# DeltaNet followed by a quick-GELU feed-forward: three feed-forward steps moved out of the second pair's hops, and dummy matmuls, conversion steps and key preparation re-dealt

## The chip, the cores and the metric

The kernel runs on one core of a Trainium2 chip. The metric is the device time of one execution in microseconds (us), as the median of several runs. A profile is one more execution with the hardware profiler on; the times inside it are counted from the start of its span.

Five engines work side by side, each through its own queue in order: TensorE (PE, matmul; its weight loads are listed apart as PEld), VectorE (DVE), ScalarE (ACT), GpSimd (POOL) and SyncE (SP, here only a queue of DMAs). They wait for each other through semaphores.

## What is computed

The reference, cut to what matters:

```python
# B, H, S, D = 4, 8, 768, 48;  d_model = H * D = 384;  d_ff = 2048
k_n = k / (norm(k, axis=-1) + 1e-6)
state = zeros((B, H, D, D))
for t in range(S):
    y[:, :, t] = q[:, :, t] @ state
    v_old = state^T k_n[:, :, t]
    state = state + beta[:, :, t] * outer(k_n[:, :, t], v[:, :, t] - v_old)
x = y.transpose(0, 2, 1, 3).reshape(B * S, H * D)       # 3072 x 384
h = x @ w_in                                            # 3072 x 2048
out = (h * sigmoid(1.702 * h)) @ w_out                  # 3072 x 384
```

So it is a recurrence over time, one per batch and head, and then a feed-forward layer on the rows that it gives. The weights w_in and w_out come in as 64-bit floats, and the kernel turns them into 32-bit floats itself.

## The kernel before

**Tiling.** Time is cut into 6 chunks of 128. A unit is a chunk and a batch: 24 units of 8 heads, numbered chunk by chunk. Inside a unit the recurrence is a triangular system, solved in 4 blocks of 32 rows. The inverses of the diagonal blocks are computed on DVE for a whole chunk (`invert`), with keys times keys (G, from PE) as input; for all chunks but the first they go out to DRAM and come back in another layout.

**Order.** All tiles that matter here are recorded through wrappers that pin an instruction to its place in the program (`pinned`, line 100), so each engine runs them in the order in which the Python code issues them. That helper has line 102, which is why the profile shows L102 nearly everywhere; groups are told apart by the tiles' names.

**Hops.** The first four units (chunk 0) are solved in two pairs (loops from lines 1021 and 1049). Each pair takes 2 x 4 hops (`hops`): in a hop one unit of the pair solves a block (psU, copied by ACT to US or U) and the other subtracts what its last solved block adds to the rows below (psR, subtracted from V by DVE). A hop needs the last hop's US and V. After a pair's hops, `put_out` computes each unit's outputs and the change of its state (psY), which ACT copies to `last` and xT and DVE adds to ST. Between a hop's instructions and those of the next hop the loops issue other work:

- `warm(n)`: n dummy matmuls of 128x256 into ps_warm, whose results nobody reads.
- `fill(n)`: n steps of the weights' conversion (`conversions`). A piece of weights takes five steps on DVE: mask the exponent into the destination (and, in the same step, a Relu on ACT that rescales it), mask the high mantissa into tmp, add the low word, join sign and exponent (this one needs the Relu), multiply. Pieces overlap by one step: the fourth step of a round begins the next piece. There are nine pieces of w_in (steps 1 to 46) and then fourteen of w_out. When a piece is done, its place may be refilled by a DMA (`fetches`).
- `ahead_of(preparing, n)`: n steps of the generator `keys`, which runs the preparation of units 4 to 8 side by side: squares on ACT (ksq), sum on DVE (ssq), a power on POOL (rn), the scaling of the keys on DVE (KN), transposes on PE (psT, copied to kT), keys times keys on PE (psG, copied to G), and the DMAs that carry G's diagonal blocks to NT (through DRAM). Here it has some 24 steps.
- `feed()`: one step of the feed-forward's first half (`hidden`): three 128x256 float matmuls (ph), which the trace shows as six; every second step also issues the gelu (gT) on ACT. The first two `hidden` take 32 feeds in all.

**Behind the hops** comes the second inverse (`inverting = invert(1)`, line 1086): 25 times a step of it and a feed, then what is left of both, then conversion steps (line 1091). Then `woven` runs over the remaining units: each call issues one step of up to three units at different stages, and spends a share of a queue of feed-forward work. The first thing in that queue is `both_written` (line 771), the second half of the feed-forward for the first two units' rows (po); it runs through w_out in sixteen parts and calls `fill` itself until the parts that it is about to need have been converted.

**PSUM.** psU, psR and psY share the four banks of ps_seq, taken in turn; psT and psG (of chunk 1) share the two of ps_big; ps_warm, ph and po the two of ps_moe.

Of the kernel before, what the change touches and what calls it, by code (L numbers as in the profile page):

```python
# [18 lines left out]
def kernel(  # L19
# [35 lines left out]
    GB = 8  # L55

    XR = DP - D
    NW, NA, NY, NU = 14, 3, 34, 11
    NQ = DFF // 4
    NPC = DFF // 8  # L60
    NS = C * C + C
# [22 lines left out]
    def load(n, pairs, dma=nc.sync.dma_start):  # L84
        c, b = units[n]
        for dst, src in pairs:
            dma(
                out=dst[n % len(dst)][:, :, 0:D],
                in_=src[b, :, c * C : (c + 1) * C, :].rearrange("h p d -> p h d"),
            )  # L90

    def load_values(n, dma=nc.sync.dma_start):
        c, b = units[n]
        V = io.tile([128, H, D], F32, tag="V", name="V", bufs=4)
        dma(
            out=V, in_=v[b, :, c * C : (c + 1) * C, :].rearrange("h p d -> p h d")
        )
        loaded[n] = V
# [33 lines left out]
    def warm(n):  # L132
        ps = ps_moe.tile([128, 256], F32, tag="moe", name="ps_warm")
        for _ in range(n):
            pe.matmul(ps, lhsT=ones[:, 0:128], rhs=ones, start=True, stop=True)
# [52 lines left out]
    def fetch_out(f):  # L188

        if f in outside:  # L190
            slot = outside[f]
            if slot not in slots:
                slots[slot] = wk.tile([128, 2 * DM], I32, tag=slot[:2].strip("2"), name="raw", bufs=3)
            words = slots[slot]
        else:
            words = raws[:, inside[f] * DM : (inside[f] + 2) * DM]
        places[f] = as_raw(words, (1, DM))
        first = order.index(f) < FC // 2
        (other_queue if first else sync)(
            out=as_rows(places[f])[:, 0], in_=moe_w_out[f * 128 : (f + 1) * 128, :]  # L200
        )
# [90 lines left out]
    def fill(n):  # L292
        for _ in range(n):
            next(converting, None)
# [459 lines left out]
    def written(c, b0, gT):  # L754

        for i in range(HB):
            b = b0 + i
            po = ps_moe.tile([128, DM], F32, tag="moe", name="po")
            for f in range(FC):
                pe.matmul(  # L760
                    po, lhsT=gT[f // FQ][:, f % FQ, i * C : (i + 1) * C], rhs=w_out[:, f, :],
                    start=(f == 0), stop=(f == FC - 1),
                )
                if f % 2 == 1 and f < FC - 1:
                    yield 1.3
            o = wk.tile([128, DM], F32, tag="o", name="o")
            act.copy(o, po)
            nc.sync.dma_start(out=out[b * S + c * C : b * S + (c + 1) * C, :], in_=o)
            yield 1.3

    def both_written(c, gT):

        po = [ps_moe.tile([128, DM], F32, tag="moe", name="po") for _ in range(HB)]
        for n, f in enumerate(order):
            ahead = order[min(n + 3, FC - 1)]
            while ("out", ahead - ahead % 2 if 4 <= ahead < 8 else ahead) not in done:
                fill(1)
            for i in range(HB):
                pe.matmul(
                    po[i], lhsT=gT[f // FQ][:, f % FQ, i * C : (i + 1) * C], rhs=w_out[:, f, :],  # L780
                    start=(n == 0), stop=(n == FC - 1),
                )
            if n < FC - 1:
                yield 1.3
        for i in range(HB):
            o = wk.tile([128, DM], F32, tag="o", name="o")
            act.copy(o, po[i])
            sync(out=out[i * S + c * C : i * S + (c + 1) * C, :], in_=o)
        yield 1.3
# [11 lines left out]
    def run(work):  # L801
        for _ in work:
            pass

    def ahead_of(work, n):
        for _ in range(n):
            next(work, None)
# [18 lines left out]
    def together(solves, belows):  # L826

        solves = [(X, blk) for X, blk in solves if X]
        belows = [(X, blk) for X, blk in belows if X]
        psU = bank("psU") if solves else None  # L830
        psR = bank("psR") if belows else None
        for h in range(H):
            for X, blk in solves:
                X.solve(blk, h, psU)
            for X, blk in belows:
                X.below(blk, h, psR)
        for X, blk in solves:
            X.solved(blk, psU)
        for X, blk in belows:
            X.rest(blk, psR)  # L840
# [157 lines left out]
    def keys():  # L998

        def unit(n):  # L1000
            yield from normalize_mixed(n)
            yield from prepare(n)

        begun[2 * B] = prepare(2 * B)

        def first(n):
            yield from normalize_mixed(n)
            next(begun[n])

        work = [unit(n) for n in range(B, 2 * B)] + [first(2 * B)]  # L1010
        for t in range(24):
            for u, begin in reversed(list(enumerate((0, 3, 6, 10, 13)))):
                s = t - begin
                if s >= 0 and s % 2 == 0:
                    next(work[u], None)
            yield
        for w in work:
            run(w)

    preparing = keys()  # L1020
    path = hops(*pair[:2])
    for i in range(2 * NB):
        together(*next(path))
        fill(2)
        if i in (3, 5):
            pair[HB + (i - 3) // 2].select()
        if i > 0:
            ahead_of(preparing, 1)
        warm(NU if i < 6 else NA)
    for n, s in enumerate(pair[:2]):  # L1030
        put_out(s, 2 - n)
        load(len(KN) + n, ((KN, k),), other_queue)
# [4 lines left out]
    def feed(n=1):  # L1037
        for _ in range(n):
            while ffn and next(ffn[0], None) is None:
                ffn.pop(0)  # L1040
# [9 lines left out]
    for i in range(2 * NB):  # L1050
        together(*next(path))
        fill(2 if i < 5 else 3)
        if i > 2:
            feed()
        else:
            warm(NU)
        ahead_of(preparing, 2)
        if 3 <= i < 6:
            fetch_out(i - 3)
        if i == 5:  # L1060
            load(B, ((QP, q),), sync)
            load_values(B, sync)
# [25 lines left out]
        ahead_of(inverting, 1)  # L1088
        feed()
    run(inverting)  # L1090
    fill(5)
    while ffn:
        feed()
    queue = [both_written(0, gTs[0]), written(*units[HB], gTs[1])]
    for n in range(B - 1, len(units) + 1):
        woven(n, 20.8 if n > 6 else 10.4)
# [32 lines left out]
```

## Time and profile before

| | us |
|---|---|
| median of 8 runs | 775.46 (773.9 to 776.14) |
| profiled execution | 775.92 |
| its span | 774.2 |
| PE busy | 750.4 (97%) |
| DVE busy | 440.5 (57%) |
| ACT busy | 240.9 (31%) |
| POOL busy | 128.5 (17%) |

Stages of the profiled execution, by the timeline of PE:

| stage | from, us | to, us |
|---|---|---|
| dummies ahead of the first hop (34) | 37.9 | 43.6 |
| first pair's hops | 43.6 | 62.9 |
| first pair's put-outs | 65.2 | 69.9 |
| second pair's hops | 69.8 | 93.9 |
| second pair's put-outs, first scores of unit 4 | 93.9 | 104.1 |
| 25 feeds (150 ph) beside the second inverse | 104.1 | 136.8 |
| second half of the feed-forward and further units | 136.6 | 774.2 |

How to read the profile: "busy" is the time in which an engine executes; matmuls are pipelined and their ends are modelled. In the row of digits the span is cut into 40 slices. In a timeline a row gives the start, the duration, the engine, the operation, what it writes and reads and how many instructions were merged; the bracket is how long the engine had been idle before and which engine's instruction ended that. PEclk is the clock granted to TensorE, 1.00 being full speed.

### The profile page before, as it was taken

Reading aid. Unit: us, or ns where it says so; the run is one execution under the profiler, and the core shown is the slowest. Engines: PE = TensorE matmul, PEld = TensorE weight load, DVE = VectorE, ACT = ScalarE, POOL = GpSimd, SP = SyncE. Lnnn points to the kernel's source line nnn. Section 1 sums busy time; section 2 is a strip of 40 time slices with the busy share of each in tenths; the row PEclk is TensorE's granted clock in tenths of the full one; section 3 lists DMA queues with packets and bytes.
Section 4 is the critical chain, followed back from the end, with each engine's and each line's share of the span. In section 5 each row is a group of like instructions: output and inputs, shape, how many; then the busy total and the mean of one; then the engine's idle time right before and its main releaser. Section 6 shows DMA issues by size and latency. Waiting matters only on the chain.

```text
span 774.2 us, 19538 instructions
## 1 busy us (share of the span) xinstructions
PE 750.4 (97%) x8537; PEld 563.6 (73%) x8537; DVE 440.5 (57%) x896; ACT 240.9 (31%) x535; POOL 128.5 (17%) x134
## 2 busy tenths in 40 slices
PE   7898999789999999999999999999999999999998
PEld 6677788456688678678678678678678677687684
DVE  6979788896965565665665665666665621000000
ACT  4564632343333223223233233223123123121110
POOL 6124210110220320220221221231210000000000
PEclk7598999999999999999999999999999999999999
DMA  9956551454342142042042042042030020000000
GB/s 158 176 73 187 120 100 33 120 131 97 76 109 56 25 105 56 22 108 57 22 99 65 22 99 65 22 99 66 22 77 12 22 44 1 17 12 1 26 1 20
DMA packets 130661, 50.78 MB, mean 66 GB/s; under 512 B 105408, under 2 KB 126016, under 8 KB 130576
## 3 DMA queue, kind: packets, MB, share of 16 engines
q1 hardware_dynamic: 128112, 41.08, 24.7%
q0 software_dynamic: 2464, 8.46, 4.5%
q8 instruction: 67, 1.10, 0.6%
q14 instruction: 18, 0.15, 0.1%
HBM read 32.08 MB, written 16.25 MB: 62 GB/s over the span
## 4 chain that ended last, share of the span: by engine, by line
PE 87%; DVE 7%; ACT 3%; DMA 2%; issue 1%; SPq 0%; DVEq 0%; ACTq 0%
PE ph L102 31%; PE po L102 30%; PE psY L102 6%; PE psU L102 5%; PE psQ L102 4%; PE psG L102 4%; PE psT L102 3%; PE psR L102 3%; DVE w_out L102 2%; DVE tmp L102 2%; ACT V L102 1%; PE ps_warm L102 1%; DVE P L102 1%; DVE V L102 1%; DMA KN<-in_k_dram 1%
## 5 line engine op out<-in xcount | busy, mean ns | idle before, releaser
L102 PE MATMUL po<-w_out,gT 128*128 128x384 f32 x768 | 267.5, 496 | 5.5 <-DVE w_out L102 5.5
L102 PE MATMUL ph<-xT,w_in 128*128 128x256 f32 x1152 | 261.1, 383 | 0.3
L102 PEld LDWEIGHTS ph<-xT,w_in 128*128 128x128 f32 x1152 | 214.9, 190 | 32.7 <-issue 1.7
L102 PEld LDWEIGHTS po<-w_out,gT 128*128 128x128 f32 x768 | 142.0, 192 | 97.2 <-DVE w_out L102 8.2
L102 DVE TENSOR_TENSOR V<-V,psR 128x384 f32<-128x384 f32 (+2 forms) x72 | 40.1, 557 | 195.7 <-PE psR L102 191.2
L102 ACT ACTIVATE gT<-ph 128x512 f32<-128x512 f32 x96 | 56.5, 596 | 144.8 <-PE ph L102 144.7
L102 DVE TENSOR_TENSOR P<-NT,YB 64x8 f32<-64x8 f32 (+26 forms) x178 | 86.4, 486 | 4.9
L102 PEld LDWEIGHTS psU<-V,XB 32*32 32x32 f32 x1536 | 59.0, 105 | 35.3 <-issue 27.6
L102 ACT COPY US<-psU 32x384 f32<-32x384 f32 x92 | 43.1, 469 | 133.0 <-PE psR L102 80.1
L102 DVE TENSOR_REDUCE YB<-P 64x4 f32<-64x8 f32 (+27 forms) x178 | 77.2, 434 | 6.1
L102 PE MATMUL psU<-V,XB 32*32 32x48 f32 x1536 | 70.4, 204 | 2.3 <-DVE V L102 2.1
L624 POOL TENSOR_SCALAR_AFFINE_SELECT M<-M 128x1024 f32<-128x1024 f32 x20 | 25.5, 1276 | 231.3 <-DVE M L102 169.3
L102 PE MATMUL psR<-US,G 32*32 32x48 f32 x2576 | 62.7, 204 | 0.9 <-ACT US L102 0.9
L102 PEld LDWEIGHTS psR<-US,G 32*32 32x32 f32 x2576 | 53.3, 104 | 2.4 <-ACT US L102 1.3
L102 PE MATMUL psQ<-QS,kT 48*128 48x176 f32 (+1 forms) x384 | 37.6, 341 | 3.7 <-ACT QS L102 3.7
L102 DVE TENSOR_TENSOR P<-NT 64x256 f32<-64x256 f32 (+7 forms) x44 | 36.3, 826 | 0.5
L102 DVE TENSOR_REDUCE NT<-P 64x64 f32<-64x1024 f32 (+7 forms) x44 | 35.3, 803 | 1.5
L102 PEld LDWEIGHTS psQ<-QS,kT 48*128 48x128 f32 x384 | 31.1, 209 | 6.8 <-ACT QS L102 5.5
L102 PE MATMUL psG<-kT 48*128 48x128 f32 x384 | 33.0, 311 | 2.7 <-ACT kT L102 1.4
L102 PEld LDWEIGHTS psG<-kT 48*128 48x128 f32 x384 | 28.0, 210 | 6.2 <-ACT G L102 2.1
L102 ACT COPY o<-po 128x384 f32<-128x384 f32 x24 | 11.5, 477 | 62.0 <-issue 39.2
L102 ACT COPY M<-psQ 128x256 f32<-128x256 f32 x68 | 22.8, 377 | 22.9 <-DVE V L102 16.8
(100 smaller groups left out, 602.7 us busy)
## 6 DMA issues: line engine op xcount, KB each, us to landing
Nd<-G SPq DMA_DIRECT2D x16, 512.0 KB, 3.5
QP<-in_q_dram SPq DMA_DIRECT2D x24, 192.0 KB, 3.8
V<-in_v_dram SPq DMA_DIRECT2D x24, 192.0 KB, 3.2
out_dram<-o SPq DMA_DIRECT2D x24, 192.0 KB, 2.4
KN<-in_k_dram POOLq DMA_DIRECT2D x15, 192.0 KB, 3.6
NT<-Nd SPq DMA_DIRECT2D x20, 128.0 KB, 2.7
Yd<-YS SPq DMA_DIRECT2D x20, 128.0 KB, 2.4
XB<-Yd SPq DMA_DIRECT2D x20, 128.0 KB, 3.4
```

What stands on the lines that cost most here:

```text
L102: return lambda *a, **kw: tc.keep_in_program_order(op(*a, **kw))
L624: (pool if self.n < B else nc.gpsimd).affine_select(out=self.M, in_=self.M, compare_op=ALU.is_gt, fill=0.0, base=0, pattern=[[0, H], [1, 1 ...
```

## The change

It does five things. Of the dummies, 26 instead of 34 go ahead of the first hop, the last two hops of the first pair get eleven each instead of three, and in the second pair hops 0 to 5 get seven each, where hops 0 to 2 had eleven. The first hop gets five conversion steps instead of two. The feeds of hops 3, 4 and 5 of the second pair are left out; they are issued after the second inverse. Hops 2 to 5 of the second pair take three steps of the keys' preparation instead of two. And the five conversion steps after the second inverse are replaced by three behind each of the feeds that are left there; with the closing turn, which finds no feed, these are twelve.

```diff
-    NW, NA, NY, NU = 14, 3, 34, 11
+    NW, NY, NU = 14, 26, 11
...
     path = hops(*pair[:2])
     for i in range(2 * NB):
         together(*next(path))
-        fill(2)
+        fill(2 if i else 5)
         if i in (3, 5):
             pair[HB + (i - 3) // 2].select()
         if i > 0:
             ahead_of(preparing, 1)
-        warm(NU if i < 6 else NA)
+        warm(NU)
...
     for i in range(2 * NB):
         together(*next(path))
         fill(2 if i < 5 else 3)
-        if i > 2:
+        if i > 5:
             feed()
         else:
-            warm(NU)
-        ahead_of(preparing, 2)
+            warm(NU * 2 // 3)
+        ahead_of(preparing, 3 if 2 <= i < 6 else 2)
...
     run(inverting)
-    fill(5)
     while ffn:
         feed()
+        fill(3)
```

## The prediction

> **What bounds the kernel now.** I read the busy slices of the page first, then the chain of waits, then clock windows, then the timelines of single engines between 42 and 176 us. Each slice below is 19.4 us, each digit a tenth.
>
> ```profile
> PE   7898999789999999999999999999999999999998
> DVE  6979788896965565665665665666665621000000
> PEclk7598999999999999999999999999999999999999
> PE 87%; DVE 7%; ACT 3%; DMA 2%; issue 1%; SPq 0%; DVEq 0%; ACTq 0%
> ```
>
> From about 176 us on TensorE (PE) sets the time without a gap, and the change touches nothing there: whatever is won or lost before 176 us arrives at the end one for one. So the question is how early the last w_out pieces are converted. The chain before that is mixed: VectorE (DVE) sets it in the first pair's hops (49 to 62 us), PE in the put-outs and the second pair's hops (62 to 104 us), PE's 25 feed-forward steps during the second inverse (104.1 to 136.8 us), then DVE converting w_out until 172 us.
>
> The granted clock (columns: PE, PEld, DVE, ACT, POOL busy; PEclk; DMA):
>
> ```profile
> 58.70:62.10 3.40, 1.44 (x35) 0.95 (x34) 3.27 (x7) 0.72 (x2) 0.18 (x1) 1.00 0.87 223
> 147.40:150.80 3.40, 1.75 (x7) 0.83 (x8) 3.26 (x7) 1.17 (x2) 0.00 (x0) 1.00 0.44 120
> 62.10:65.50 3.40, 3.39 (x27) 2.74 (x29) 3.37 (x5) 1.77 (x3) 1.31 (x1) 0.51 0.88 196
> 65.50:68.90 3.40, 3.40 (x43) 3.40 (x43) 2.71 (x5) 1.57 (x5) 1.54 (x2) 0.50 0.29 48
> ```
>
> A stretch of 3.4 us with PE busy for 1.44 was followed by half clock for 6.8 us, one with 1.75 busy was not. PE's timeline shows the cause and the cost:
>
> ```profile
> 59.80 0.50 PE L102 MATMUL ps_warm<-ident 128*128 128x256 bf16 x3
> 62.11 1.49 PE L102 MATMUL psU<-V,XB 32*32 32x48 f32 x16 [1.81 <-DVE V L102]
> 63.53 1.12 PE L102 MATMUL psT<-ident,KN 128*128 128x128 f32 x4
> ...
> 69.81 0.86 PE L102 MATMUL psU<-V,XB 32*32 32x48 f32 x16
> 70.61 1.38 PE L102 MATMUL ps_warm<-ident 128*128 128x256 bf16 x11
> ```
>
> After three dummy matmuls PE waited 1.81 us for DVE, and the same 16 psU take 1.49 there and 0.86 at full clock.
>
> DVE, early and behind the inverse (the bracket is idle time and its releaser):
>
> ```profile
> 43.02 0.93 DVE L102 TENSOR_SCALAR tmp<-w_out 128x768 int32<-128x768 int32 x1
> 47.89 0.55 DVE L102 TENSOR_TENSOR V<-V,psR 128x384 f32<-128x384 f32 x1 [3.94 <-ACT w_in L102]
> ...
> 133.47 0.36 DVE L102 TENSOR_SCALAR tmp<-raw 128x384 int32<-128x384 int32 x1
> 138.36 0.55 DVE L102 TENSOR_REDUCE ssq<-ksq 128x8 f32<-128x384 f32 x1 [4.54 <-ACT ksq L102]
> ```
>
> ScalarE (ACT) holds that ksq back, because the squares stand behind the last gelu, which waits for PE's last feed:
>
> ```profile
> 136.82 0.60 ACT L102 ACTIVATE gT<-ph 128x512 f32<-128x512 f32 x1 [1.93 <-PE ph L102]
> 137.31 0.60 ACT L102 ACTIVATE w_out<-w_out,low 128x384 int32<-128x384 int32 x1
> 137.82 0.51 ACT L102 ACTIVATE ksq<-KN 128x384 f32<-128x384 f32 x1
> ```
>
> **The change, part by part.** A "step" is one step of the conversion, nearly always one DVE instruction; five make a piece, one of them also sends a Relu to ACT.
>
> *NY 34 to 26.* Eight dummies of 0.125 us (1.37 for eleven) go before the first hop. That hop starts some 1 us sooner, but the next one needs US, which ACT copies only behind the 32 scalings of V (38.56 to 45.88). Gain 0. PE now idles about 0.4 + 1.0 = 1.4 us there; a 3.4 us stretch around it is still busy for 2.0, above the 1.75 that kept the clock.
>
> *Five steps in the first hop.* DVE was idle 3.94 us before its subtraction at 47.89. Steps 3 (0.9) and 4 (0.7) fit into that. Step 5 needs the Relu that ACT starts at 46.14 (0.93), so it runs 47.1 to 48.07 and the subtraction is 0.18 late. From there to the subtraction at 61.49 DVE does ten steps in both versions, two whole pieces, so the same work; only a wait of 0.29 us at 52.5 goes. Gain 0.1, bounds -0.2 (the wait stays) and 0.6 (steps pack at the shortest spacing seen, 0.87 instead of 0.97).
>
> *Eleven dummies in the last two hops of the first pair.* The eight added ones before the wait take 1.0 of its 1.81 us. The stretch is then busy for 1.44 + 1.0 = 2.4 of 3.4 us: full clock stays. At full clock psU, psT, eleven dummies and the 64 psY come to 0.8 + 0.45 + 1.3 + 2 x 1.48 = 5.5 us (1.48 is the later put-out's 32 psY), against 69.81 - 62.11 = 7.7. That is 2.2 if nothing else binds. But conversion is three steps further on and so is ACT's queue: in ACT's order the next Relu and the kT copy now stand ahead of the first put-out's copies, and that Relu waits for DVE's 19th step, some 4.1 us after the last subtraction; DVE's ST addition, which frees the PSUM bank of the next hop, follows about 2.7 us behind it. This puts the second pair's first psU near 68.5, not 67.5. Gain 1.2; bounds 2.2 and a loss of 1.2 (see the second rival).
>
> The Trainium skill, "TensorE: Matmul & The Clock Gate", section "Why this matters for your kernels", asks only that PE have no idle gaps above about 3 us. By that the 1.81 us gap would have been harmless and the eight dummies worth nothing, which would take 1.2 from the sum; the half clock in the rows decides against it. The same page ("What's actually happening") says that the activity window runs freely, at no fixed place against the kernel; no row here shows more than one execution, so some of the timed runs may never have had the fall, and the gain with it.
>
> *Second pair's hops.* Three feeds of 1.49 us leave hops 3 to 5 (4.5). Three times eleven dummies at 1.31 become six times seven at about 0.85 (net +1.2). With three preparation steps in hops 2 to 5, each psG there is followed at once by a psT, which must wait for ACT's copy of G as at 80.26 (0.68); two more such waits and moved transposes cost 1.6. PE's sum from psU at 69.81 to the last hop at 93.08 falls by 4.5 - 1.2 - 1.6 = 1.7 us. DVE takes part of it back. Its work is the same 19 steps, seven subtractions and four norms, 19.5 us busy, but three norm stages come sooner: the second norm waits about 0.4 for POOL's power (1.66), and between the last two subtractions three steps of 768 columns and the subtraction itself need 3.0 us where PE now asks for 1.7. Gain 0.9, bounds 0 (DVE paces every hop) and 1.7.
>
> The keys' DMAs to and from DRAM move with the preparation: the last NT load was issued at 96.16 and takes 3.1 us, against a first use at 104.57, so it is not late even if it keeps its place. On POOL the four w_out fetches (2.38) pass ahead of the two KN loads (0.96 and 0.90); those keys are squared more than 4 us after they land at present, which hides that.
>
> *Put-outs of the second pair.* Same PE work. ACT now has the Relu of w_out's first and second pieces ahead of the copies and of QS; I take 0.3 us of loss (bounds 0, 1.0).
>
> *Behind the inverse.* The three feeds run here: 28 instead of 25, at 32.64/25 = 1.306 us, so PE ends 36.6 us after it starts instead of 32.6. DVE's inverse takes 27 us from nearly the same moment. Before, five steps followed and then the 4.54 us stall, and the sixth step ran at 138.83. Now three of the five are already done (in the 1.8 us that DVE idled before 103.64), and twelve follow. Nine run at once; the tenth needs a Relu behind the 15th gelu: after 26 feeds, 33.95 + 0.5 + 0.6 = 35.1 us after PE's start. Two more steps, then the ssq waits for the squares behind the 16th gelu and another Relu: 36.6 + 0.5 + 0.5 + 0.6 = 38.1. With 104.14 as start the next step (the 63rd) runs at 142.75; before it ran at 143.22. Gain 0.5. The 3.9 us added to PE are hidden by its slack in the conversion that follows: between 136.8 and 172 PE has 56 po at 0.32 (1.29 for four), and about 7 us of hops, psQ, psG and psT, 25 of 35 us. Without that cover they cost 3.9.
>
> *Sum.* -0.1 - 1.2 - 0.9 + 0.3 - 0.5 = -2.4 us. The profiled execution took 775.92 (span 774.2), so 773.5 for it; it lay 0.46 above the median 775.46, which gives 773.1.
>
> **Rivals.** *Nothing binds but PE:* DVE and ACT keep up, gains 0.6 + 2.2 + 1.7 + 0.5 = 5.0, time 770.5. For it: DVE idles 3.8 us in the second hops. Against: a subtraction stands behind three long steps.
>
> *The clock falls anyway:* if DVE is late by another 0.6 us or more at 61.5, busy time drops back under 1.75. Then the eleven dummies before the put-out run at half clock, 2.3 against the 0.64 of the three, and the second pair starts 1.2 late; the other terms bring back 0.1 + 0.9 - 0.3 + 0.5. Time 775.46, no change. For it: DVE's queue is full there.
>
> *The moved feeds are paid (slower):* if PE, not DVE, limits the stretch to 172 us, the 3.9 us come in full instead of the 0.5 gained: -1.9 + 3.9 = +2.0, time 777.5. It decides from the point where PE's slack behind the feeds falls under 3.9; I count about 10. For it: the page's 97% PE. Against: the 5.5 us that PE waits on w_out.
>
> **How the numbers follow.** Forecast 53%, nothing binds 15%, clock falls 20%, feeds paid 12%. 0.2% is 1.55 us, about what a measurement of this kernel can tell from no change. The forecast's own range is 772 to 774.3, of which some 85% lies under 773.9. Of the second rival 0.02 falls on faster and 0.03 on slower. Faster: 0.53 x 0.85 + 0.15 + 0.02 = 0.62; slower: 0.12 + 0.03 = 0.15; the rest, 0.23, the same. The range 770.5 to 776.3 takes in the first rival and the second with a margin, and leaves most of the third out.
>
> **What would show it.** Clock 1.0 from 62 to 69 us; the second pair's first psU near 68.5; the long run of ph starting near 102.2 with 168 matmuls, not 150; DVE stalls of about 4 and 1.5 us behind the inverse, not one of 4.5; the conversion ending near 169.6. Wrong if PE has no gaps waiting for w_out any more, if a half-clock stretch stands elsewhere, or if the run of ph starts where it did.

## The result, and the profile after

The changed kernel takes 781.14 us in the median of 21 runs (774.65 to 790.31); the kernel before takes 775.25 (57 runs). The ratio is 1.0061, with a 95% interval of 1.0045 to 1.0077: slower by 0.6%, where 773.1 was predicted. Two runs, 787.66 and 790.31, lie so far above the fastest that they count as slow; the ratio leaves them out, and it is smaller than that of the medians (1.0076). The profiled execution took 781.68, its span 780.0. The spread is far wider than before (there 54 of 57 runs lie between 771.94 and 776.26), and it follows the mean clock that TensorE was granted: runs with 0.978 took 774.65 to 775.48, with 0.967 778.83 to 781.14, with 0.958 785.78. One and the same program loses the clock for a longer or shorter time from run to run.

From the page after, the busy slices of PE and DVE, the granted clock, and the chain's shares:

```profile
PE   7898999999999999999999999999999999999998
DVE  5998569796976565666666666665665531000000
PEclk8599589999999999999999999999999999999999
PE 87%; DVE 8%; ACT 3%; issue 1%; POOL 0%; DVEq 0%; POOLq 0%; ACTq 0%
```

The chain's shares are nearly as before. PE's dip in the eighth and ninth slices is gone (9 and 9, before 7 and 8). The clock row shows the loss: before, the fourth slice had a digit of 8, with the first pair's put-outs; now the fifth, where the second pair's hops are, is at half speed (5) and the sixth has an 8. (The 5 in the second slice is in both.) Behind the last of the three marks in the table below, both kernels need the same: 601.0 us before, 600.4 now.

The windows of the same execution, in stretches of 3.4 us (columns: PE, PEld, DVE, ACT, POOL busy; PEclk; DMA):

```profile
75.60:79.00 3.40, 2.22 (x62) 1.75 (x59) 1.82 (x4) 3.07 (x7) 1.64 (x1) 1.00 0.15 22
79.00:82.40 3.40, 2.72 (x21) 2.08 (x20) 2.49 (x7) 1.09 (x3) 0.72 (x1) 0.50 0.29 66
82.40:85.80 3.40, 3.40 (x58) 2.63 (x58) 1.02 (x2) 1.22 (x3) 2.55 (x4) 0.50 0.47 67
89.20:92.60 3.40, 3.40 (x42) 2.64 (x42) 1.00 (x2) 1.26 (x3) 0.00 (x0) 0.50 0.22 41
96.00:99.40 3.40, 3.40 (x22) 2.45 (x21) 3.33 (x5) 1.41 (x2) 0.00 (x0) 0.50 0.49 83
```

and in stretches of 1 us:

```profile
102.00:103.00 1.00, 1.00 (x14) 1.00 (x12) 0.00 (x0) 0.29 (x1) 0.00 (x0) 0.54 0.67 147
103.00:104.00 1.00, 1.00 (x23) 0.93 (x20) 0.00 (x0) 0.45 (x2) 0.00 (x0) 1.00 0.61 246
```

The clock halves at 79.0 and is back only at 102.9, 23.9 us later, although PE is recorded as busy for all of 3.40 us in the third to fifth rows. PE's timeline:

```profile
61.14 0.86 PE L102 MATMUL psU<-V,XB 32*32 32x48 f32 x16 [1.08 <-DVE V L102]
...
62.42 1.36 PE L102 MATMUL ps_warm<-ident 128*128 128x256 bf16 x11
...
67.05 0.86 PE L102 MATMUL psU<-V,XB 32*32 32x48 f32 x16 [0.45 <-ACT xT L102]
...
74.62 1.16 PE L102 MATMUL psG<-kT 48*128 48x128 f32 x16
76.96 0.66 PE L102 MATMUL psT<-ident,KN 128*128 128x128 f32 x4 [1.18 <-ACT G L102]
...
78.36 1.07 PE L102 MATMUL ps_warm<-ident 128*128 128x256 bf16 x7
79.36 2.08 PE L102 MATMUL psG<-kT 48*128 48x128 f32 x16
```

Up to 78 us the change does what was predicted: the first pair's last psU runs at full clock (0.86, before 1.49), PE's wait there is 1.08 instead of 1.81, and the second pair starts at 67.05 instead of 69.81. Then psT waits 1.18 us for ACT's copy of G, the clock falls, and the same psG that takes 1.16 takes 2.08.

Three marks divide the rest: the second pair's first psU, the start of the long run of ph, and the psG behind the last Relu of w_out, which ends the conversion. Their distances, from the timelines of PE, for all kernels of this study (the runs are described below):

| kernel | pair 2 to ph | ph to end of conversion | median | kernel before, timed with it |
|---|---|---|---|---|
| before | 34.3 | 69.1 | 775.25 | |
| changed | 44.0 | 68.6 | 781.14 | 775.25 |
| e1 feeds back | 38.0 | 68.1 | 776.76 | 774.33 |
| e2 feeds moved only | 33.8 | 72.4 | 776.53 | 774.33 |
| e3 eleven dummies | 36.6 | 68.6 | 776.44 | 774.33 |
| e4 first pair only | 34.3 | 67.7 | 771.17 | 774.33 |
| f1 e4, 26 dummies | 34.3 | 67.8 | 771.75 | 774.91 |
| f2 e4, feeds out, woven | 33.9 | 68.6 | 772.81 | 774.91 |
| f3 e4, keys sooner | 36.5 | 67.7 | 774.49 | 774.91 |
| f4 f2 with seven dummies | 40.3 | 68.5 | 773.80 | 774.91 |
| g1 f2, keys sooner | 36.2 | 68.5 | 774.33 | 774.59 |
| g2 e4, eight steps | 34.3 | 66.5 | 769.60 | 774.59 |
| h1 e4's dummies only | 35.0 | 69.1 | 772.33 | 774.59 |
| h2 e4's steps only | 34.3 | 67.7 | 771.97 | 774.59 |

### The profile page after: what moved, and what is told of

Read it like the earlier page. It is cut to its first block, busy times and chain, and to the rows that moved or that the text cites. A ratio compares the mean times of both kernels' runs of the same rounds, so it can differ in the third digit from the quotient of the medians.

```text
span 780.0 us, 19566 instructions
## 1 busy us (share of the span) xinstructions
PE 757.6 (97%) x8554; PEld 568.6 (73%) x8554; DVE 440.2 (56%) x896; ACT 240.7 (31%) x535; POOL 130.3 (17%) x134
## 4 chain that ended last, share of the span: by engine, by line
PE 87%; DVE 8%; ACT 3%; issue 1%; POOL 0%; DVEq 0%; POOLq 0%; ACTq 0%
PE ph L102 32%; PE po L102 30%; PE psY L102 6%; PE psU L102 5%; PE psQ L102 4%; PE psG L102 4%; PE psT L102 3%; PE psR L102 2%; DVE w_out L102 2%; DVE tmp L102 2%; DVE w_in L102 1%; PE ps_warm L102 1%; ACT V L102 1%; DVE V L102 1%; DVE P L102 1%
## 5 line engine op out<-in xcount | busy, mean ns | idle before, releaser
L102 PE MATMUL psG<-kT 48*128 48x128 f32 x384 | 33.9, 317 | 2.7 <-ACT kT L102 1.5
L87 POOL DMA_DIRECT2D KN<-in_k_dram x13 | 12.4, 953 | 106.2 <-PE psY L102 97.2
```

What stands on the lines that cost most here:

```text
L87: dma(out=dst[n % len(dst)][:, :, 0:D], in_=src[b, :, c * C : (c + 1) * C, :].rearrange("h p d -> p h d"),)
L102: return lambda *a, **kw: tc.keep_in_program_order(op(*a, **kw))
```

## The experiments

### The change with one part taken back, and two parts alone

e1 puts the feeds of hops 3 to 5 back into the changed kernel, e2 takes only those feeds out of the kernel before, e3 raises the changed kernel's dummies, e4 makes only the first pair's edits.

```diff
 # e1, from the changed kernel
-        if i > 5:
+        if i > 2:
             feed()
 # e2, from the kernel before
-        if i > 2:
+        if i > 5:
             feed()
 # e3, from the changed kernel
-            warm(NU * 2 // 3)
+            warm(NU)
 # e4, from the kernel before
-        fill(2)
+        fill(2 if i else 5)
...
-        warm(NU if i < 6 else NA)
+        warm(NU)
```

> The changed kernel with the feeds of hops 3 to 5 of the second pair put back (seven dummies only in hops 0 to 2); everything else as changed. Theory A (without the float matmuls of the feeds PE is too lightly used in these hops, so the clock falls there and stays at half for some 20 us): clock 1.0 from 62 to 104 us, the long run of ph starts near 102, about 773, and the spread of the runs is that of the kernel before. Theory B (the preparation taken sooner does it: psT right behind psG waits for ACT's copy of G, the squares wait for keys that land late, and these gaps drop the clock): the gaps and the half clock stay, 778 or more. Theory C (the three feeds cost 3.9 us behind the inverse): 777.

Measured: 776.76, 775.09 to 784.05 over 12 runs, ratio 1.0048 (1.0023 to 1.0072). The long run of ph starts at 105.3, not near 102; in the profile the clock is halved only from 79.6 to 83.0. With the feeds the clock is back sooner there, but the kernel is still slower than before, and four of its runs take 779.28 to 784.05. Neither theory A nor B holds by itself.

> The kernel before with one edit: hops 3 to 5 of the second pair issue eleven dummies instead of a feed, so three feeds come after the second inverse. Theory A: the clock falls in the second pair's hops in many runs, 778 or more with a wide spread. Theory B: preparation is as before, so no fall, 774 to 776. Theory C: no fall, but PE ends 3.9 us later behind the inverse, 779, with a narrow spread.

Measured: 776.53, 775.39 to 777.77, ratio 1.0032 (1.002 to 1.0043). The spread is narrow and the clock does not fall in the hops, so with eleven dummies in their place the feeds are not missed: theory A in its first form falls. But the stage behind the inverse is 3.4 us longer (72.4 against 69.1): DVE's wait there for ACT's squares grows from 4.54 to 7.92 us:

```profile
140.75 0.55 DVE L102 TENSOR_REDUCE ssq<-ksq 128x8 f32<-128x384 f32 x1 [7.92 <-ACT ksq L102]
```

Without conversion steps between them the moved feeds are paid for, nearly in full. In the hops 0.5 us comes back (33.8 against 34.3).

> The changed kernel with eleven dummies instead of seven in hops 0 to 5 of the second pair, 0.48 us each of added PE work, 2.9 in all. Theory A: fewer falls of the clock than in the changed kernel; the median goes to about 777, and the best runs are some 2 to 3 us slower than the best of the changed kernel. Theory B: the gaps stay, so the median rises to 783 or so. Theory C: 784.

Measured: 776.44, 772.78 to 781.2, ratio 1.0029 (1.0008 to 1.005). Better than the changed kernel by 4.7 us, with four more dummies per hop, as theory A has it. But theory A's best runs, 2 to 3 us slower than the best of the changed kernel, did not come: the best is 1.9 us faster (772.78 against 774.65), so even the best runs of the changed kernel were probably not free of falls. The profile shows full clock in the second pair's hops, but now half clock from 47.2 to 57.4 us, a second place at which the change loses it (columns as above):

```profile
43.60:47.00 3.40, 2.56 (x90) 2.10 (x88) 3.33 (x5) 3.37 (x10) 0.73 (x1) 1.00 1.26 137
47.00:50.40 3.40, 3.40 (x92) 2.51 (x91) 2.51 (x4) 1.17 (x3) 0.00 (x0) 0.53 0.12 20
```

> The kernel before with only the first pair's edits: five conversion steps in the first hop, eleven dummies in hops 6 and 7 (34 dummies ahead as before). Theories A, B and C alike: the half-clock stretch from 62 to 69 us goes, the second pair starts 1.5 to 2.5 us sooner, and the time is 773 to 774.

Measured: 771.17, ratio 0.9965 (0.9946 to 0.9985). That is 2 us better than the 773 to 774 expected. The half-clock stretch from 62 to 69 us is gone, the second pair starts at 68.05 instead of 69.81, and the conversion ends 1.35 us sooner behind the inverse.

### One part at a time on top of the first pair's edits

```diff
 # f1
-    NW, NA, NY, NU = 14, 3, 34, 11
+    NW, NA, NY, NU = 14, 3, 26, 11
 # f2
-        if i > 2:
+        if i > 5:
             feed()
...
-    fill(5)
     while ffn:
         feed()
+        fill(3)
 # f3
-        ahead_of(preparing, 2)
+        ahead_of(preparing, 3 if 2 <= i < 6 else 2)
 # f4: f2, and
-            warm(NU)
+            warm(NU * 2 // 3)
```

> The first pair's edits (as in the fourth run) plus 26 dummies instead of 34 ahead of the first hop. The third run showed a half-clock stretch from 46 to 56 us with 26 dummies. Theory A (every place where PE is thinly used for some 3.4 us can lose the clock, and where the free-running window falls decides it from run to run): the median 771 to 772.5, but some runs 3 to 6 us up, a wider spread than 769.5 to 773.1 of the fourth run. Rival (26 dummies cost nothing): 771.2 with the same spread.

Measured: 771.75, ratio 0.9968 (0.9943 to 0.9992), in two groups: seven runs from 769.98 to 771.78 and five from 773.93 to 777.38. The profile has half clock from 47.9 to 51.2. PE's timeline of f1:

```profile
46.07 0.29 PE L102 MATMUL psR<-US,G 32*32 32x48 f32 x8 [1.46 <-ACT US L102]
...
47.46 2.20 PE L102 MATMUL ps_warm<-ident 128*128 128x256 bf16 x11
```

PE waits 1.46 us for ACT, which copies US only behind its scalings of V, and the dummies that follow take 2.20 instead of 1.38. Fewer dummies move the first hop up, but not the next one; they only lengthen PE's wait. This fall is cheap: the profiled run took 771.73, one of the faster group, and its second pair starts 0.7 us later than e4's. Where the five slower runs lost their time no profile shows; their mean clock is 0.967 to 0.973, but so is that of e4's three slowest (773.0 to 777.47). Against e4 the median shows no price of the eight dummies.

> The first pair's edits plus: feeds of hops 3 to 5 left out (eleven dummies in their place), and three conversion steps behind each of the feeds left after the inverse. Theory A with eleven dummies enough: PE's hops 0.5 us shorter in all, the conversion ends about where it did, 770.5 to 772, no wide spread. Theory A with eleven too few: falls in the second pair's hops, 773 or more and wide. Theory C (the feeds are paid behind the inverse although the conversion is woven in): 774 to 775, narrow.

Measured: 772.81, 771.99 to 773.67, ratio 0.9964 (0.9948 to 0.998), the narrowest spread of all. The profile has no fall in the hops. (It has 3.4 us of half clock from 171.5 on. So have 11 of the 14 profiles somewhere between 140 and 185 us, the kernel before twice; the mean clock of a run does not tell at which of these places it lost the clock.) Leaving the feeds out and weaving the conversion in is worth nothing against e4 (0.4 us shorter hops, 0.8 longer behind them), and costs little; theory C's 774 to 775 does not come, and the 770.5 to 772 of theory A is missed by 0.8.

> The first pair's edits plus three preparation steps instead of two in hops 2 to 5 of the second pair. Theory B (the keys taken sooner bring psT right behind psG, so PE waits for ACT's copy of G, 0.7 us and more in each of hops 2 to 4, and late keys hold ACT up): the long run of ph starts 2 to 3 us later than in the fourth run, 773.5 to 775, with some falls. Theory A alone: 771 to 772.

Measured: 774.49, 771.59 to 776.6, ratio 0.9986 (0.9965 to 1.0007): the first pair's gain is nearly gone. The run that was profiled kept its clock, so it shows the price without a fall: 2.2 us between the second pair's start and the ph. The waits in the second pair's hops (engine and what it waited for: us in total, times, longest), of f3 first:

```profile
PE psT L102 <- ACT G L102: 2.3, 3, 0.9
ACT ksq L102 <- DMA KN<-in_k_dram: 1.1, 1, 1.1
```

and of e4:

```profile
PE psT L102 <- ACT G L102: 0.7, 1, 0.7
ACT ksq L102 <- DMA KN<-in_k_dram: 0.8, 1, 0.8
```

Three hops instead of one have psT right behind psG, and PE waits 1.6 us longer for the copies. Theory B's gaps are real. The seven runs from 774.49 up have mean clocks of 0.971 to 0.976, the five others 0.979 to 0.982, which suggests that some runs lose the clock on top; none of the seven was profiled.

> The second kernel of this call with seven dummies instead of eleven in hops 0 to 5. Theory A: falls in the second pair's hops come back in many runs, 773 to 778 and wide, while runs without a fall are 2 us faster than those with eleven. Theory B: without the sooner keys there are no gaps and no falls, 769.5 narrow.

Measured: 773.8, 770.61 to 781.21, ratio 0.9984 (0.9955 to 1.0014). It differs from f2 by four dummies in each of six hops. Three runs, at 770.6 to 770.9, are 2 us faster than f2, as theory A has it; the profiled one (777.98) has half clock from 78.4 to 95.5. PE's timeline of f4:

```profile
73.59 0.94 PE L102 MATMUL ps_warm<-ident 128*128 128x256 bf16 x7
74.58 1.16 PE L102 MATMUL psG<-kT 48*128 48x128 f32 x16
77.47 0.66 PE L102 MATMUL psT<-ident,KN 128*128 128x128 f32 x4 [1.74 <-ACT G L102]
```

Here the keys are not taken sooner, and the fall comes all the same. In both, ACT has waited for a load of keys before it copies G (1.29 us in f2, 1.26 in f4). With eleven dummies that costs PE little (f2's psT waits 0.78); faster by the missing dummies, PE reaches psT earlier and waits 1.74 us. With the feeds out, seven dummies instead of eleven are enough for the fall.

### The whole change with safe dummies, the first pair's edits apart, and a better version

g1 is f2 with f3's edit: the changed kernel, but for 34 dummies ahead and eleven per hop. h1 and h2 are the two edits of e4 each by itself. g2 is e4 with this:

```diff
-    fill(5)
+    fill(8)
     while ffn:
```

> The changed kernel but for its two thin dummies: 34 instead of 26 ahead of the first hop, eleven instead of seven in hops 0 to 5 of the second pair. Theory A with the price of the keys (1.6 to 2.2 us of waits for ACT's copy of G, seen in the seventh run): the long run of ph starts 2 us later than in the sixth run (feeds out, woven), median 774 to 775.5; how many of its runs lose the clock tells whether those waits are enough for it at eleven dummies. If theory A alone were right: 772.8 as the sixth.

Measured: 774.33, 773.28 to 775.14, ratio 0.9993 (0.9976 to 1.0009). None of its 11 runs lies more than 0.8 us above the median. The windows of g1 over the stretch in which the changed kernel fell:

```profile
75.60:79.00 3.40, 2.72 (x71) 2.22 (x70) 1.34 (x3) 2.82 (x6) 1.64 (x1) 1.00 0.22 31
79.00:82.40 3.40, 2.72 (x30) 2.21 (x31) 2.98 (x7) 1.68 (x4) 0.16 (x1) 1.00 0.43 78
```

PE waits here too, but less (busy for 2.72 of 3.40 us, where the changed kernel had 2.22), and it holds the clock. So everything in the change but the two smaller counts of dummies comes to no difference, and those counts make the loss: 781.14 - 775.25 against 774.33 - 774.59, 5.9 against -0.3 us in medians. e3 has one of the two counts put back, and g1 differs from it in the dummies ahead of the first hop alone: e3 lies 2.1 us above its kernel before, with runs up to 781.2, g1 0.3 below, with none above 775.14. By these differences, which are estimates, the 26 dummies cost about 2.4 us and the seven per hop about 3.8. No run has the seven with 34 ahead and the rest of the change.

> The kernel before with only the dummies of hops 6 and 7 of the first pair raised from three to eleven. If the half clock at 62 to 69 us was the price of PE's wait there: most of the fourth run's gain, 772 to 773. If the conversion steps made the gain: 775 or above, since eleven dummies cost 0.7 us more before the put-out.

Measured: 772.33, ratio 0.9973 (0.9961 to 0.9985), as expected if the half clock was the price of PE's wait. In the profile that wait is 0.94 us instead of 1.81, the clock is full from 42 to 146 us, and the second pair starts at 67.06.

> The kernel before with only the five conversion steps in the first hop. The steps alone take three of DVE's behind the inverse away (1.35 us there in the fourth run), the half clock at 62 to 69 us stays: 773 to 774. If the steps alone made the whole gain: 771.

Measured: 771.97, ratio 0.9964 (0.9952 to 0.9977), better than the 773 to 774 expected. In the profile the half clock lasts from 62.3 to 65.7 only. Each edit alone gives 2.3 to 2.6 us and both together 3.2: they do not add up.

> The first pair's edits, with eight conversion steps instead of five behind the second inverse. In the fourth run DVE idles 4.5 us there, waiting for squares on ACT that stand behind the last gelu. Three steps (0.56, 0.36 and 0.56 us, no new Relu) fit into that, so the conversion should end 1.4 us sooner, 769.8 against 771.2. If the conversion does not set the time any more there: 771.2.

Measured: 769.60, ratio 0.9938 (0.9926 to 0.995), as expected (769.8); it is the fastest kernel of this study and faster than both kernels of the case. DVE's timeline of e4 behind the inverse:

```profile
131.50 0.55 DVE L102 SCALAR_TENSOR_TENSOR w_out<-raw,w_out 128x384 int32<-128x384 int32 x1
136.59 0.55 DVE L102 TENSOR_REDUCE ssq<-ksq 128x8 f32<-128x384 f32 x1 [4.54 <-ACT ksq L102]
```

and of g2:

```profile
136.93 0.55 DVE L102 TENSOR_REDUCE ssq<-ksq 128x8 f32<-128x384 f32 x1 [2.95 <-ACT ksq L102]
```

The three steps take 1.6 us of the wait, and the conversion ends 1.25 us sooner after the start of ph.

## Why the prediction was wrong

**The step that failed** is the one on the second pair's hops: "Gain 0.9, bounds 0 (DVE paces every hop) and 1.7". It summed PE's time at full clock and never asked whether the clock would hold there. Between the second pair's start and the ph the changed kernel needs 44.0 us where 34.3 minus 0.9 plus 0.3 were forecast. Set against g1 (36.2), which issues 24 more dummies in these hops (some 2.9 us at 1.31 for eleven), the half clock costs up to 7.8 + 2.9 = 10.7 us in the profiled execution; this is an estimate from above, since f4's best runs gained only 2 us over f2 by the same 24 dummies. With those 2 us off g1's 36.2, the stage would have taken some 34.2 us at full clock, still 0.5 more than forecast. The clock was named as a rival, but only for the first pair's end, where it did not fall; a half-clock stretch elsewhere was named as a sign of being wrong, and it came.

**Behind it lies a wrong measure.** From two stretches the prediction took busy time as the test: 1.44 of 3.4 us lost the clock, 1.75 kept it. After the change the stretch with 2.22 lost it, and stretches recorded as busy throughout did not bring it back. Near the first hops, e3 lost it behind 2.56 us and the changed kernel kept it with 2.59 (44.9 to 48.3). Recorded busy time does not decide it alone; what PE does seems to count too: in the stretch from 82.4 it ran psU, psR, psT and six dummies, and the clock came back only behind a stretch of ph and psY.

**26 dummies, "gain 0":** right for the time of the hops, wrong for the risk. The prediction counted 2.0 us of busy time around the longer gap as safe. f1 lost the clock there behind a stretch with 1.96, e3 behind the one with 2.56, and e3 against g1 puts the price at about 2.4 us. Beside the first pair's edits alone (f1 against e4) the medians show none.

**First pair: right in kind, too small in size.** The second pair's start was forecast near 68.5 and came at 67.05; the bank wait on the put-out's copies was there (0.45 us), smaller than feared. The part is worth 3.2 us by itself (e4), where 1.3 and a share of the 0.5 behind the inverse were put down for it.

**Keys sooner:** the price of the psT waits, 1.6 us, was right (f3: 2.3 against 0.7), but the change was not charged with all of it: the preparation costs 2.2 us with the feeds in place (f3 against e4) and 2.3 without (g1 against f2). The prediction saw that four w_out fetches pass ahead of the two loads of keys (KN) on POOL, and took that to be hidden, since the squares come "more than 4 us after they land". It is not hidden. ACT's second ksq, before and after:

```profile
76.82 0.52 ACT L102 ACTIVATE ksq<-KN 128x384 f32<-128x384 f32 x1
75.27 0.52 ACT L102 ACTIVATE ksq<-KN 128x384 f32<-128x384 f32 x1 [0.71 <-DMA KN<-in_k_dram]
```

Behind the fetches the loads take 6.3 to 7.0 us to land, before 3.6 to 4.5. ACT's wait holds up the copy of G for which PE idles 1.18 us right ahead of the fall. The five steps in the first hop bring this, not the preparation: h2, with them alone, waits 0.6 us (loads 7.0 to 7.1), h1, without them, does not (4.1 to 4.9). f2 kept the clock in spite of a wait of 1.29, so the late keys alone do not make the fall; no run tries the changed kernel with early keys.

**Behind the inverse: right.** Forecast were stalls of about 4 and 1.5 us, 168 ph, and 0.5 us gained; the step after them was to come 38.6 us behind the start of the ph (142.75 with 104.14 as start) and came at 38.58. (The sum 36.6 + 0.5 + 0.5 + 0.6 there makes 38.2, not 38.1; nothing hangs on it.) DVE's timeline after:

```profile
146.21 0.56 DVE L102 SCALAR_TENSOR_TENSOR w_out<-raw,w_out 128x384 int32<-128x384 int32 x1 [3.63 <-ACT w_out L102]
...
149.15 0.55 DVE L102 TENSOR_REDUCE ssq<-ksq 128x8 f32<-128x384 f32 x1 [1.52 <-ACT ksq L102]
```

The stage takes 68.57 instead of 69.06 us: 0.49. What the prediction did not see is where it comes from: the three steps taken early in the first hop gain 1.34 us by themselves (e4, h2), and of that the moved feeds, though woven in, cost 0.84 again (f2 against e4). Without the weaving they cost 3.4 us (e2). The slower rival, with its 777.5, had the sign right for another cause; as a mechanism it did not happen.

**The Trainium skill** ("TensorE: Matmul & The Clock Gate", section "Why this matters for your kernels") asks for no idle gaps above about 3 us. Here gaps of 1.18, 1.46 and 1.74 us preceded falls, so by these measurements the limit is too wide for such thinly used stretches. Its other statement, in "What's actually happening", that the activity window runs freely, fits: by their times and mean clocks, the runs of one kernel lose the clock for different lengths of time (f1, f4, the changed kernel).

Open stays how the chip weighs kinds of matmuls in its window; no run here isolated a single kind. That the run-to-run spread comes from the window's phase fits the two groups of times, but the phase itself was not set by any run.

## What to carry to other kernels

Dummy matmuls, or real ones, between short dependent steps hold the clock up: before thinning them out, look at each stretch of some 3.4 us that is left (half clock came in multiples of that length here) and at what kinds of matmul are in it, and read several runs, since one profile shows one of them. Thinning can cost more than it saves: with 24 dummies fewer, three runs of f4 are 2 us faster than f2's median and the slowest is 8 us slower. When an engine idles because its input stands in another engine's queue behind something late, first fill that wait with work that needs nothing from that queue (g2: three steps, 1.6 us).

## What the runs showed of the hardware that was not expected

Half clock can last: 23.9 us in the changed kernel with PE recorded as busy for 27.6 of 30.2 us around it (72.2 to 102.4). Its lengths behind the first matmuls are 3.4 (h2, f1, e1), 6.8 (before), 10.2 (e3), 17.1 (f4) and 23.9 us (changed), all multiples of 3.41. With the feeds out, the number of dummies that holds the clock in these hops lies between seven and eleven of 128x256 in bf16 (f4's profile fell; f2's and g1's did not, and their 11 runs each lie within 1.9 us of each other). The same program's runs then differ by up to 2% (774.65 to 790.31), and the best of them are no proof of a gain.
